# GpSimd's shifted passes as 64-bit additions, squares and normalising multiplies on VectorE

## The chip, the cores and the metric

One core of one Trainium2 chip runs the program. The metric is the device time in microseconds; three runs of the kernel before give 697.55 (696.05 to 713.22). A NeuronCore has TensorE (PE) for matrix products, ScalarE (ACT) for exponentials, VectorE (DVE) and GpSimd (POOL) for elementwise work, and SyncE (SP), whose queue issues the DMAs here. PE writes to PSUM, which has eight banks of 128 x 512 float32; the other operands lie in SBUF.

## The reference

A transformer block with attention and a feed-forward part side by side, both on the same normalised input:

```python
xn = layernorm(x)                         # x: 2048 x 640, no scale or shift
q = (xn @ wq), 32 heads of 20;  k = xn @ wk;  v = xn @ wv     # one k and v for all heads
p = softmax(q k^T / sqrt(20))             # 32 heads x 2048 x 2048
attn = (p v, heads side by side) @ wo
h = relu(xn @ w1 + b1);  ffn = (h * h) @ w2 + b2              # 1536 hidden
return x + attn + ffn
```

The 32 x 2048 x 2048 exponentials are the bulk of the elementwise work.

## The kernel before

The scores are computed transposed: 128 keys on the partitions, 512 queries along the free dimension. A block is four heads (a group) for 512 queries; there are 4 x 8 = 32 blocks. In a block there are 16 tiles of 128 keys, each with four score matrices of 128 x 512, one for each head: 512 tiles, 2048 matrices. The four heads use different rows of PE, so up to four score matrices run side by side as one batch (L1301). The product with v (PV, L1783) has four heads side by side in four column ranges and sums over the tiles of a block in one PSUM bank; v has a column of ones, which gives the sum of the exponentials.

A tile goes one of two ways.

- *ACT's way*: the exponential (L1485) over two or three matrices in neighbouring banks, from PSUM to the ring PT, and then one PV group of four matmuls.
- *VectorE's way*: q is scaled so that a score, plus an offset and converted to a 16-bit integer, is the bit pattern of a bfloat16 power of two with a mantissa that is linear in between (L1581, one conversion for each head, from PSUM into the buffer pbx). The error of the linear mantissa is evened out by four such patterns: the first and three that are shifted by an added 32, 64 and 96 (`PH_D`), each with a weight that lies in its copy of v (`vp`, `PH_W`). A shifted pass adds the constant to all 2048 patterns of a tile (four heads x 512). So the tile has four PV groups. pbx holds ten such sets of patterns.

Of the three shifted passes of a tile VectorE does two (L1602) and GpSimd one (L1664), unless the block is almost over, when VectorE does all (`share` false). A pass that GpSimd does not come to is taken back by VectorE (`S_STEAL`) when more than `PHQ` are queued. GpSimd also squares the ReLU's result (L1094, 48 tiles of 128 x 512) and multiplies the attention's sums by the broadcast reciprocal (L1844, 29 blocks; the last three blocks go another way on VectorE).

VectorE's fast passes from SBUF to SBUF and GpSimd use one port of SBUF, so the program lets GpSimd work only while VectorE reads PSUM. `pieces` and `cut` cut a GpSimd instruction to the length of the VectorE instruction (or two) that it is laid beneath; what is left becomes another piece.

Nothing of this order is decided on the chip. A planner in the file (`Sched`) runs through the whole kernel with a duration for each instruction, picks at each step the request that can start first on each engine (priorities break ties), and writes out a fixed list for each engine with the semaphore waits. Its choices hang on constants: `PHP_F + PHP_E * n` is the planned time of a shifted pass of n patterns on GpSimd; `MAXD` tiles in a block at most go VectorE's way, and `claim` takes one when the rest of the block is longer than `clt` plus VectorE's backlog; `OPN` is how many matrices of claimed tiles may be left when the next one is claimed. `PLAN` holds thirteen further values for each half block: among them `give`, how many of VectorE's matrices may be outstanding, `dstarv` and `hungw`, the backlogs below which a score batch takes more of VectorE's matrices and fewer of ACT's, `await_`, how much later than the batch a PSUM bank may come free and still be counted, and `p1tol`, how late a conversion may be before it is put first. `S_QK` composes the batches from these: two or three matrices for ACT, the rest for VectorE, each in a bank of its own.

```python
if na and len(units) > 2 and len(long_held()) < 4 and not (wanted[0] and pos() < EARLY) and (F >= 5 or F >= 4 and not starving or F == 3 and not hungry):
    a = 3
```

Of the kernel before, what the change touches and what calls it, by code (L numbers as in the profile page):

```python
# [8 lines left out]
I16 = mybir.dt.int16  # L9
ALU = mybir.AluOpType  # L10
# [36 lines left out]
OPN = 1  # L47
# [4 lines left out]
NPB = 10  # L52
PHQ = 2
PHP_F, PHP_E = 156.0, 0.836
OVER = 40.0
# [32 lines left out]
PLAN = [dict(zip(PLAN_KEYS, p)) for p in (  # L88
    (620.0, 3500.0, 600.0, 6000.0, 300.0, 900.0, 12, 1, 0.3, 3, 60.0, 300.0, 4.0),
    (620.0, 3500.0, 600.0, 6000.0, 300.0, 900.0, 12, 1, 0.0, 3, 60.0, 300.0, 1.9),  # L90
    (650.0, 3500.0, 600.0, 6000.0, 300.0, 900.0, 15, 2, 0.0, 3, 0.0, 300.0, 4.0),
    (580.0, 3500.0, 600.0, 6000.0, 300.0, 900.0, 10, 2, 0.0, 3, 150.0, 300.0, 4.0),
    (650.0, 3500.0, 600.0, 9000.0, 300.0, 900.0, 12, 2, 0.0, 3, 60.0, 300.0, 4.0),
    (650.0, 4000.0, 600.0, 6000.0, 150.0, 900.0, 12, 2, 0.0, 4, 0.0, 300.0, 4.0),
    (680.0, 3500.0, 600.0, 6000.0, 300.0, 900.0, 12, 2, 0.0, 3, 60.0, 300.0, 4.0),
    (650.0, 3500.0, 600.0, 6000.0, 300.0, 900.0, 12, 2, 0.0, 3, 60.0, 300.0, 4.0),
    (650.0, 3500.0, 600.0, 6000.0, 0.0, 900.0, 12, 2, -0.3, 3, 60.0, 300.0, 4.0),
    (650.0, 3500.0, 600.0, 6000.0, 0.0, 900.0, 10, 2, -0.3, 3, 60.0, 300.0, 4.0),
    (650.0, 3500.0, 600.0, 6000.0, 0.0, 900.0, 12, 2, 0.0, 3, 60.0, 300.0, 1.9),
    (650.0, 3500.0, 600.0, 6000.0, 0.0, 900.0, 14, 2, 0.0, 4, 60.0, 0.0, 4.0),  # L100
    (760.0, 3500.0, 600.0, 6000.0, 0.0, 900.0, 14, 2, 0.0, 4, 60.0, 0.0, 4.0),
    (760.0, 3500.0, 600.0, 6000.0, 300.0, 900.0, 14, 2, 0.0, 2, 60.0, 600.0, 4.0),
    (760.0, 3500.0, 600.0, 6000.0, 300.0, 900.0, 14, 2, 0.0, 2, 60.0, 600.0, 4.0),
    (620.0, 3500.0, 600.0, 6000.0, 300.0, 900.0, 12, 2, 0.3, 3, 60.0, 300.0, 1.9),
    (650.0, 3500.0, 600.0, 6000.0, 300.0, 900.0, 12, 2, 0.0, 3, 60.0, 0.0, 4.0),
    (650.0, 3500.0, 600.0, 6000.0, 150.0, 900.0, 12, 2, 0.0, 2, 60.0, 300.0, 4.0),
    (650.0, 3500.0, 600.0, 6000.0, 150.0, 900.0, 15, 2, 0.3, 2, 60.0, 300.0, 4.0),
    (650.0, 3500.0, 900.0, 6000.0, 150.0, 1200.0, 12, 2, 0.0, 3, 60.0, 300.0, 4.0),
    (650.0, 3500.0, 600.0, 6000.0, 300.0, 900.0, 12, 2, 0.0, 3, 60.0, 300.0, 4.0),
    (620.0, 2600.0, 600.0, 6000.0, 300.0, 900.0, 12, 2, 0.0, 2, 60.0, 300.0, 4.0),  # L110
    (620.0, 2200.0, 600.0, 6000.0, 300.0, 900.0, 12, 2, 0.0, 2, 60.0, 300.0, 4.0),
    (650.0, 3500.0, 600.0, 6000.0, 300.0, 900.0, 12, 2, 0.0, 3, 60.0, 300.0, 4.0),
    (650.0, 3500.0, 600.0, 6000.0, 300.0, 900.0, 12, 2, 0.0, 3, 60.0, 300.0, 4.0),
    (650.0, 3500.0, 600.0, 9000.0, 300.0, 900.0, 10, 2, 0.0, 3, 60.0, 300.0, 4.0),
    (650.0, 3500.0, 600.0, 9000.0, 300.0, 900.0, 10, 2, 0.0, 3, 60.0, 600.0, 1.9),
    (620.0, 3500.0, 600.0, 6000.0, 300.0, 1200.0, 12, 3, 0.0, 3, 60.0, 300.0, 4.0),
    (650.0, 3500.0, 600.0, 6000.0, 300.0, 900.0, 12, 2, 0.0, 3, 60.0, 300.0, 4.0),
    (580.0, 3500.0, 600.0, 6000.0, 300.0, 900.0, 12, 2, 0.0, 3, 60.0, 300.0, 4.0),
    (650.0, 3500.0, 600.0, 6000.0, 300.0, 900.0, 12, 2, 0.0, 3, 60.0, 300.0, 4.0),
    (650.0, 3000.0, 600.0, 6000.0, 300.0, 900.0, 12, 2, 0.0, 3, 60.0, 300.0, 4.0),  # L120
    (650.0, 3500.0, 600.0, 6000.0, 300.0, 900.0, 12, 2, 0.0, 3, 60.0, 0.0, 4.0),
    (720.0, 3500.0, 600.0, 6000.0, 300.0, 900.0, 12, 2, 0.0, 3, 60.0, 600.0, 4.0),
    (720.0, 3500.0, 600.0, 6000.0, 300.0, 900.0, 12, 2, 0.0, 3, 60.0, 600.0, 4.0),
    (650.0, 3500.0, 600.0, 6000.0, 300.0, 900.0, 12, 2, 0.0, 3, 60.0, 300.0, 4.0),
    (650.0, 2200.0, 600.0, 6000.0, 300.0, 900.0, 12, 2, 0.0, 3, 60.0, 300.0, 4.0),
    (620.0, 3500.0, 600.0, 6000.0, 300.0, 900.0, 12, 2, 0.0, 3, 60.0, 300.0, 4.0),
    (620.0, 3500.0, 600.0, 6000.0, 300.0, 900.0, 12, 1, 0.0, 3, 0.0, 300.0, 4.0),
    (650.0, 3500.0, 600.0, 6000.0, 300.0, 900.0, 12, 2, 0.0, 3, 60.0, 300.0, 4.0),
    (650.0, 3500.0, 600.0, 7500.0, 150.0, 900.0, 14, 2, 0.0, 3, 0.0, 300.0, 4.0),
    (650.0, 3500.0, 600.0, 6000.0, 300.0, 900.0, 12, 2, 0.0, 3, 60.0, 300.0, 4.0),  # L130
    (760.0, 3500.0, 600.0, 6000.0, 300.0, 900.0, 12, 2, 0.0, 3, 60.0, 0.0, 4.0),
    (760.0, 3500.0, 600.0, 6000.0, 300.0, 900.0, 12, 2, 0.0, 3, 60.0, 0.0, 4.0),
    (650.0, 3500.0, 600.0, 9000.0, 300.0, 900.0, 12, 2, 0.0, 3, 60.0, 0.0, 4.0),
    (650.0, 3500.0, 600.0, 6000.0, 300.0, 900.0, 12, 2, 0.0, 3, 60.0, 300.0, 4.0),
    (650.0, 3000.0, 600.0, 6000.0, 300.0, 1200.0, 12, 2, 0.0, 3, 150.0, 300.0, 4.0),
    (760.0, 3500.0, 600.0, 6000.0, 150.0, 900.0, 12, 2, 0.0, 3, 60.0, 300.0, 4.0),
    (620.0, 3500.0, 600.0, 6000.0, 300.0, 900.0, 12, 2, 0.0, 3, 60.0, 300.0, 4.0),
    (720.0, 3500.0, 600.0, 6000.0, 300.0, 900.0, 12, 2, 0.0, 3, 0.0, 0.0, 4.0),
    (620.0, 3500.0, 600.0, 6000.0, 300.0, 1200.0, 12, 2, 0.0, 3, 60.0, 300.0, 4.0),
    (650.0, 3500.0, 600.0, 6000.0, 300.0, 900.0, 12, 2, 0.0, 3, 60.0, 0.0, 4.0),  # L140
    (650.0, 3500.0, 600.0, 6000.0, 300.0, 900.0, 12, 2, 0.0, 3, 60.0, 0.0, 4.0),
    (650.0, 3500.0, 600.0, 6000.0, 150.0, 900.0, 12, 2, 0.0, 2, 60.0, 0.0, 4.0),
    (650.0, 3500.0, 600.0, 6000.0, 150.0, 900.0, 12, 2, 0.0, 3, 60.0, 600.0, 4.0),
    (650.0, 3500.0, 600.0, 6000.0, 300.0, 900.0, 12, 2, 0.0, 3, 60.0, 300.0, 4.0),
    (650.0, 3500.0, 600.0, 6000.0, 0.0, 900.0, 12, 2, 0.0, 3, 60.0, 300.0, 1.9),
    (650.0, 3500.0, 600.0, 6000.0, 150.0, 900.0, 15, 2, 0.0, 3, 60.0, 300.0, 4.0),
    (650.0, 2200.0, 600.0, 6000.0, 300.0, 900.0, 14, 2, 0.0, 3, 60.0, 300.0, 4.0),
    (650.0, 3500.0, 600.0, 6000.0, 300.0, 900.0, 12, 2, 0.0, 3, 60.0, 300.0, 4.0),
    (720.0, 3500.0, 600.0, 6000.0, 300.0, 1200.0, 12, 2, 0.0, 3, 60.0, 300.0, 4.0),
    (650.0, 3500.0, 600.0, 6000.0, 300.0, 900.0, 12, 2, 0.0, 3, 60.0, 300.0, 4.0),  # L150
    (650.0, 3500.0, 600.0, 6000.0, 300.0, 900.0, 12, 2, 0.0, 3, 60.0, 300.0, 4.0),
    (650.0, 3500.0, 600.0, 6000.0, 300.0, 900.0, 12, 2, 0.0, 3, 60.0, 300.0, 4.0),
)]
PAAT = 24.7
PAQ = ()
NPX = 1
PQAT = (7.0, 10.5)
PQSTEP = .3
XRP = 2.0
# [1910 lines left out]
```

## Time and profile before

| | |
|---|---|
| median of the runs | 697.55 us |
| span of the profiled execution | 694.0 us |
| TensorE clock granted | 1.00 throughout |
| exponentials (L1485) | 688: 596 over two matrices, 92 over three |
| conversions (L1581) | 564 instructions for 580 matrices, that is 145 tiles |
| shifted passes on VectorE (L1602) | 302 |
| pieces of shifted passes on GpSimd (L1664) | 510, in 17 lengths |
| squares on GpSimd (L1094) | 85 pieces, 55.4 us |
| normalising multiplies on GpSimd (L1844) | 40 pieces, 32.1 us, and a few more |
| PV matmuls (L1783) | 1468 with PT, 1740 with pbx and vp, 580 with pbx and vx |

The last column of a group's line says how long its engine stood idle just before these instructions and what ended that. A matmul's duration includes the time that it takes to run through PE, so groups of matmuls overlap; what a group costs PE is the distance from its start to the next one's. The same holds to a lesser degree on VectorE: a conversion takes 0.68 us and the next instruction starts 0.60 after it.

### The profile page before, as it was taken

To read this page: it belongs to the slowest core of one execution; us is meant where nothing else is said; L and a number is where in the kernel's file an instruction comes from. 1 tells how busy PE (TensorE), PEld (TensorE's weight loads), DVE (VectorE), ACT (ScalarE), POOL (GpSimd) and SP (SyncE) were. 2 spreads that over 40 slices of the span, in tenths; PEclk is the share of its full clock that TensorE was granted. 3 is DMA by queue.
4 is the path that set the end of the run, shared out by engine and by line. 5 is a ranking of instruction groups with operands and counts; after the bars stand their busy time and mean duration, and the time that the engine had idled before them with its cause. 6 is when DMAs were issued, how large, how long until landed. Compare 5 with 4: busy or idle time off the path is not lost.

```text
span 694.0 us, 23288 instructions
## 1 busy us (share of the span) xinstructions
PE 681.5 (98%) x9825; PEld 222.6 (32%) x9825; DVE 657.9 (95%) x1141; ACT 679.1 (98%) x710; POOL 428.9 (62%) x698
## 2 busy tenths in 40 slices
PE   8999999999999999999999999999999999999997
PEld 5332222222223333332223333333222333333334
DVE  7979999999999999989999999999999999999985
ACT  6999999999999999999999999999999999999995
POOL 2866566766666666667765666676776566655510
PEclk9999999999999999999999999999999999999999
DMA  7362233101101111211100111111110111121001
GB/s 218 77 163 61 61 85 93 29 15 32 24 18 22 33 45 22 47 43 23 26 13 20 44 30 42 33 24 43 28 26 19 22 37 33 31 56 33 12 2 41
DMA packets 39891, 29.89 MB, mean 43 GB/s; under 512 B 23562, under 2 KB 34795, under 8 KB 39787
## 3 DMA queue, kind: packets, MB, share of 16 engines
q1 hardware_dynamic: 39787, 28.39, 17.3%
q8 instruction: 79, 1.29, 0.8%
q14 instruction: 25, 0.20, 0.1%
HBM read 11.12 MB, written 2.62 MB: 20 GB/s over the span
## 4 chain that ended last, share of the span: by engine, by line
PE 59%; ACT 35%; DVE 3%; POOL 1%; DMA 0%; issue 0%; DVEq 0%
ACT PT L1485 35%; PE ps L1783 22%; PE ps L1301 19%; PE ps L950 17%; DVE stats L696 1%; POOL big L731 1%; DVE pbx L1581 0%; DMA pbx<-in_A_x_dram 0%; DVE pbx L1602 0%; POOL vp L1002 0%; DVE hT_tmp L1086 0%; DVE out_sb L1144 0%; POOL pbx L1664 0%; PE ps L939 0%; DVE Rb L806 0%
## 5 line engine op out<-in xcount | busy, mean ns | idle before, releaser
L1485 ACT ACTIVATE PT<-ps 128x1024 bf16<-128x1024 f32 (+1 forms) x688 | 672.4, 1139 | 2.5 <-PE ps L1301 2.3
L1664 POOL TENSOR_SCALAR pbx<-pbx 128x576 int16<-128x576 uint16 (+16 forms) x510 | 314.0, 636 | 173.1 <-DVE pbx L1602 172.0
L1581 DVE TENSOR_SCALAR pbx<-ps 128x512 int16<-128x512 f32 (+1 forms) x564 | 377.3, 696 | 20.1 <-PE ps L1301 18.1
L1301 PE MATMUL ps<-qT,kT 20*128 20x512 bf16 x2048 | 268.7, 384 | 3.0 <-ACT PT L1485 1.4
L1602 DVE TENSOR_SCALAR pbx<-pbx 128x2048 int16<-128x2048 int16 x302 | 206.5, 708 | 1.7 <-POOL big L731 0.8
L1783 PE MATMUL ps<-pbx,vp 128*32 128x512 bf16 x1740 | 157.6, 383 | 1.1 <-POOL vp L1002 0.8
L1301 PEld LDWEIGHTS ps<-qT,kT 20*128 20x128 bf16 x2048 | 67.2, 91 | 259.3 <-ACT PT L1485 185.4
L1783 PE MATMUL ps<-PT,vx 128*32 128x512 bf16 x1468 | 141.6, 383 | 0.2
L950 PE MATMUL ps<-w_sb,big 128*32 128x320 bf16 x1536 | 81.4, 302 | 0.0
L950 PE MATMUL ps<-xnT,w_sb 128*32 128x512 bf16 x960 | 77.1, 384 | 0.5 <-DVE pbx L1581 0.4
L1094 POOL TENSOR_TENSOR big<-hT_tmp 128x256 bf16<-128x256 bf16 (+5 forms) x85 | 55.4, 667 | 22.7 <-DVE pbx L1602 22.2
L1783 PE MATMUL ps<-pbx,vx 128*32 128x512 bf16 x580 | 56.8, 384 | 0.8 <-ACT PT L1485 0.4
L1783 PEld LDWEIGHTS ps<-pbx,vp 128*32 128x32 bf16 x1740 | 41.6, 95 | 48.6 <-issue 33.8
L1783 PEld LDWEIGHTS ps<-PT,vx 128*32 128x32 bf16 x1468 | 37.4, 95 | 43.1 <-issue 33.5
L950 PEld LDWEIGHTS ps<-w_sb,big 128*32 128x32 bf16 x1536 | 31.4, 95 | 32.7 <-issue 25.6
L1844 POOL TENSOR_TENSOR OTs<-Tn,Rb 128x224 bf16<-128x224 f32 (+5 forms) x40 | 32.1, 811 | 15.7 <-DVE pbx L1602 15.7
L1086 DVE TENSOR_SCALAR hT_tmp<-ps,b1col 128x512 bf16<-128x512 f32 x48 | 35.4, 737 | 0.7 <-PE ps L950 0.7
L950 PE MATMUL ps<-wo_p,OTp 120*32 120x320 bf16 (+1 forms) x640 | 34.9, 302 | 0.0
L950 PE MATMUL ps<-xnT,wq_sb 128*32 128x512 bf16 x375 | 31.1, 383 | 0.0
L950 PEld LDWEIGHTS ps<-xnT,w_sb 128*32 128x32 bf16 x960 | 18.9, 94 | 28.8 <-issue 21.1
L1783 PEld LDWEIGHTS ps<-pbx,vx 128*32 128x32 bf16 x580 | 14.9, 94 | 18.3 <-issue 13.1
L1828 DVE COPY Tn<-ps 128x512 f32<-128x512 f32 x29 | 19.7, 680 | 0.1
(95 smaller groups left out, 197.2 us busy)
## 6 DMA issues: line engine op xcount, KB each, us to landing
Rb<-Rr SPq DMA_DIRECT2D x29, 256.0 KB
xres<-in_A_x_dram SPq DMA_DIRECT2D x16, 160.0 KB, 4.1
out_dram<-out_sb SPq DMA_DIRECT2D x16, 160.0 KB, 2.3
qT<-qpk SPq DMA_DIRECT2D x105, 20.0 KB
pbx<-in_A_x_dram SPq DMA_DIRECT2D x3, 640.0 KB
w_sb<-in_B_w_dram SPq DMA_DIRECT2D x1, 1920.0 KB
OTp<-OTs SPq DMA_DIRECT2D x96, 20.0 KB
w_sb<-in_B_w_dram SPq DMA_DIRECT2D x4, 480.0 KB
```

What stands on the lines that cost most here:

```text
L696: v = yield (lambda hh=hh: Req(("dve", 400.0, 470.0, [lambda e: e.bn_stats(out=stats6[:, st, hh, :], in_=x_sb[:, st, 320 * hh:320 * hh + 3 ...
L950: return lambda e: e.matmul(ps[32 * j:32 * j + m, b_[0], 0:n], Lj, R, start=first, stop=last, tile_position=(0, 32 * j))
L1086: v = yield Req(("dve", 658.0, 742.0, [lambda e: e.tensor_scalar(out=hT_tmp[:, k, :], in0=ps[:, b_[0], :], scalar1=b1col[:, f:f + 1], scal ...
L1094: w = yield from pieces(512, 139.0, 1.7, lambda c0, c1: (lambda e: e.tensor_tensor(out=h2T[:, qc % 2, f, c0:c1], in0=hT_tmp[:, k, c0:c1], ...
L1301: ins.append(lambda e, i=i, b=b, t=t, h=h: e.matmul(ps[:, i, :], kT[32 * h:32 * h + DH, t * 128:(t + 1) * 128], qT[32 * h:32 * h + DH, b % ...
L1485: op = yield Req(("act", d_, d_ + 107.0, [lambda e, slot=slot, n=n, src=src: e.activation(out=PT[:, slot:slot + n, :], in_=ps[:, src, :], ...
L1581: return Req(("dve", d_, d_ + 82.0, [lambda e: e.tensor_scalar(out=PB[:, k, hsl, :], in0=ps[:, bk:bk + np_, :], scalar1=OFFS, scalar2=0.0, ...
L1602: return Req(("dve", 600.0, 684.0, [lambda e: e.tensor_scalar(out=PB[:, k, :, :], in0=PB[:, s, :, :], scalar1=PH_D[j], scalar2=None, op0=A ...
L1664: return lambda e: e.tensor_scalar(out=PB[:, k, :, :].rearrange("p h n -> p (h n)")[:, c0:c1], in0=PBU[:, s, :, :].rearrange("p h n -> p ( ...
L1783: ins = [(lambda e, h=h, first=first, last=last: e.matmul(ps[32 * h:32 * h + 32, bk, :], lhs, rhs[h], start=first, stop=last, tile_positio ...
L1828: v = yield Req(("dve", 600.0, 682.0, [lambda e: e.tensor_copy(out=Tn[:, tb, :], in_=ps[:, pvb, :])]), (lambda: None if oldt() is None els ...
L1844: w = yield from pieces(512, 138.0, 2.14, lambda c0, c1: (lambda e: e.tensor_tensor(out=dst[:, c0:c1], in0=Tn[:, tb, c0:c1], in1=Rb[:, a, ...
```

## The change

Four things are changed.

1. A shifted pass on GpSimd is one 64-bit integer addition for each four neighbouring 16-bit patterns (`int64_add`), with the constant repeated in all four; no pattern gets near a carry. Its planned time is 180 + 0.425 n ns. Until the layernorm and the weighted copies of v are done GpSimd keeps to the old form.
2. VectorE does 0.3 of a tile's three passes itself (`DPH`), that is none or one, instead of two; the others are queued for GpSimd, each with its index j.
3. The squares and the normalising multiplies become whole VectorE instructions.
4. The planner's values change: one set for all half blocks (`dstarv` 0, `p1tol` 300, `give` 5, `await_` 150, the rest as most of the 64 sets had them), `OPN` 3, `LATE` 0.5.

```diff
-OPN = 1
+OPN = 3
+I64_F, I64_E = 180.0, 0.425
+DPH = 0.3
+SQ_D, SQP, NM_D, NMP = 330.0, 3, 600.0, 2
-PLAN = [dict(zip(PLAN_KEYS, p)) for p in (
-    (620.0, 3500.0, 600.0, 6000.0, 300.0, 900.0, 12, 1, 0.3, 3, 60.0, 300.0, 4.0),
...
-)]
+PLAN = [dict(zip(PLAN_KEYS, (650.0, 3500.0, 0, 6000.0, 300.0, 300, 12, 2, 0.0, 5, 150, 300.0, 4.0)))] * 64
-LATE = 0.2
+LATE = 0.5
+        PB8 = pbx[:, :].bitcast(U64).rearrange("p (k w) -> p k w", k=NPB)
...
         def sq(qc, f, k, v, old):
-            w = yield from pieces(512, 139.0, 1.7, lambda c0, c1: (lambda e: e.tensor_tensor(out=h2T[:, qc % 2, f, c0:c1], in0=hT_tmp[:, k, c0:c1], in1=hT_tmp[:, k, c0:c1], op=ALU.mult)),
-                                  [v] + old, 1, f"SQ{qc}_{f}")
+            w = yield Req(("dve", SQ_D, SQ_D + 82.0, [lambda e: e.tensor_tensor(out=h2T[:, qc % 2, f, :], in0=hT_tmp[:, k, :], in1=hT_tmp[:, k, :], op=ALU.mult)]),
+                          [v] + old, SQP, f"SQ{qc}_{f}", port=True)
...
                 share = left_ns(b) >= PHT and b < NBLK - 1
-                if share:
-                    php.append((n, b, t, s, acc, left))
-                for j in range(NPH - 1 if share else NPH):
+                own = int((n + 1) * DPH) - int(n * DPH) if share else NPH
+                for j in range(own, NPH):
+                    php.append((n, b, t, s, acc, left, j))
+                for j in range(own):
                     cur = [None]
                     op = yield (lambda: ph_req(cur, n, b, t, s, acc, j))
...
-                def part(c0, c1, k, s):
+                def part(c0, c1, k, s, j, wide):
+                    if wide:
+                        return lambda e: e.int64_add(PB8[:, k, c0 // 4:c1 // 4], PB8[:, s, c0 // 4:c1 // 4], int(PH_D[j]) * 0x0001000100010001)
...
-                    c1 = cut(2048, PHP_F, PHP_E)
+                    wide = have(*[f"VP{c}" for c in range(4)], *[f"X{st}" for st in range(ST)])
+                    F_, E_ = (I64_F, I64_E) if wide else (PHP_F, PHP_E)
+                    n, b, t, s, acc, left, j = php[0]
+                    c1 = cut(2048, F_, E_)
...
-            w = yield from pieces(512, 138.0, 2.14, lambda c0, c1: (lambda e: e.tensor_tensor(out=dst[:, c0:c1], in0=Tn[:, tb, c0:c1], in1=Rb[:, a, c0:c1], op=ALU.mult)),
-                                  (lambda: None if own and free() is None else [done[f"dc{b}"]] + old() + (free() if own else [])), 0, f"N3_{b}")
+            w = yield Req(("dve", NM_D, NM_D + 82.0, [lambda e: e.tensor_tensor(out=dst[:, :], in0=Tn[:, tb, :], in1=Rb[:, a, :], op=ALU.mult)]),
+                          (lambda: None if own and free() is None else [done[f"dc{b}"]] + old() + (free() if own else [])), NMP, f"N3_{b}", port=True)
```

## The prediction

> **What bounds the kernel now.** The page comes first: three engines are busy for nearly the whole span, and a busy share alone cannot say which one paces the rest.
>
> ```profile
> PE 681.5 (98%) x9825; PEld 222.6 (32%) x9825; DVE 657.9 (95%) x1141; ACT 679.1 (98%) x710; POOL 428.9 (62%) x698
> ...
> L1485 ACT ACTIVATE PT<-ps 128x1024 bf16<-128x1024 f32 (+1 forms) x688 | 672.4, 1139 | 2.5 <-PE ps L1301 2.3
> L1664 POOL TENSOR_SCALAR pbx<-pbx 128x576 int16<-128x576 uint16 (+16 forms) x510 | 314.0, 636 | 173.1 <-DVE pbx L1602 172.0
> L1581 DVE TENSOR_SCALAR pbx<-ps 128x512 int16<-128x512 f32 (+1 forms) x564 | 377.3, 696 | 20.1 <-PE ps L1301 18.1
> ...
> L1602 DVE TENSOR_SCALAR pbx<-pbx 128x2048 int16<-128x2048 int16 x302 | 206.5, 708 | 1.7 <-POOL big L731 0.8
> ```
>
> ACT's exponentials stood idle 2.5 us in all, VectorE's conversions 20 us. The table by stretches says that this is so in the steady part too:
>
> ```profile
> 500.00:600.00 100.00, 99.80 (x1482) 32.08 (x1484) 96.00 (x159) 100.00 (x103) 65.46 (x106) 1.00 0.13 28
> ```
>
> (columns: length, then PE, PEld, DVE, ACT, POOL, granted clock, DMA share, GB/s.) PE's 99.80 could be modelled ends, so I read the starts in the timeline of PE:
>
> ```profile
> 501.52 0.39 PE L1301 MATMUL ps<-qT,kT 20*128 20x512 bf16 x3
> 501.85 0.40 PE L1783 MATMUL ps<-pbx,vx 128*32 128x512 bf16 x4
> 502.07 0.60 PE L1783 MATMUL ps<-pbx,vp 128*32 128x512 bf16 x8
> 502.61 0.39 PE L1301 MATMUL ps<-qT,kT 20*128 20x512 bf16 x2
> 502.93 0.40 PE L1783 MATMUL ps<-pbx,vx 128*32 128x512 bf16 x4
> 503.27 0.39 PE L1301 MATMUL ps<-qT,kT 20*128 20x512 bf16 x4
> 503.59 0.61 PE L1783 MATMUL ps<-pbx,vp 128*32 128x512 bf16 x8
> ```
>
> Two PV groups follow each other at 0.22 us; a score batch takes 0.32 to 0.33 us to the next group **whether it holds 2, 3 or 4 matrices**, and the group ahead of it takes 0.32 to 0.34 instead of 0.22. So a batch costs PE 0.32 + 0.10 = 0.42 us however full it is. Groups of 320 columns start 0.14 apart. The ledger: 688 batches (one for each exponential) x 0.42 = 289; PV (1740 + 1468 + 580)/4 = 947 groups, with 240 of FFN, 98 of Q and 15 of K 1300 x 0.22 = 286; 576 groups of 320 columns x 0.14 = 81; 20 us of start. That is 676 of 694: **PE has some 18 us of slack, ACT and VectorE have as little.** All three are bounds at once.
>
> **What one VectorE tile is worth.** Of 512 score tiles 580/4 = 145 go by VectorE's patterns: four conversions (L1581) and three shifted passes, which make four PV groups instead of one. A tile moved from ACT to VectorE saves ACT 4 x 0.43 and costs PE 3 x 0.22 = 0.66 us; it saves PE 0.42 for each batch that goes away. At before's 1468/688 = 2.13 matrices to an exponential a tile takes away 4/2.13 = 1.9 batches, 0.79 us. So freeing VectorE relieves ACT, but PE only by 0.13 us a tile. **PE gains only if batches get fuller.**
>
> **The parts.**
>
> Price of an addition of 2048 patterns on POOL. The trace has no 64-bit addition. The rows nearest to it:
>
> ```profile
> L1664 POOL TENSOR_SCALAR pbx<-pbx 128x576 int16<-128x576 uint16 x153 | 102.2, 670 | 88.0 <-DVE pbx L1602 87.7 <-DVE pbx L1581 0.2
> L1094 POOL TENSOR_TENSOR big<-hT_tmp 128x512 bf16<-128x512 bf16 x11 | 11.4, 1040 | 8.4 <-DVE pbx L1602 8.4
> L1844 POOL TENSOR_TENSOR OTs<-Tn,Rb 128x512 bf16<-128x512 f32 x6 | 7.7, 1276 | 4.8 <-DVE pbx L1602 4.8
> L1664 POOL TENSOR_SCALAR pbx<-pbx 128x2048 int16<-128x2048 uint16 x3 | 5.7, 1897 | 0.7 <-DVE pbx L1602 0.7
> ...
> L1873 DVE TENSOR_TENSOR T<-Tn,rd 128x512 bf16<-128x512 f32 x2 | 1.4, 681 | 0.0
> ```
>
> (1897 - 670)/(2048 - 576) = 0.83 ns an element; starts of neighbours are 36 ns nearer than durations, so a pass is 0.15 + 0.83 x 2048 = 1.86 us. With one such step for each 64-bit element (512 of them) it would be 0.58; with two steps, one for each 4-byte word, 1.00; at the slowest row (L1844 with 320 to 512 elements, 2.1 ns an element) for each word, 2.3. I take the planner's 180 + 0.425 x 2048 = 1.05: next to the two-step figure, and its constants for the three kinds of POOL instruction shown (0.836, 1.7, 2.14 ns an element) are within 3% of their rows.
>
> POOL loses the squares and the normalising multiplies: 55.4 + 32.1 us and smaller groups, about 95. On VectorE the 29 multiplies cost by L1873, whose successor starts 82 ns before its end, 0.60 each: 17 us. The 48 squares have both inputs in SBUF in bf16: at most L1873's 0.60 (29 us), at least 0.16 (L1833's spacing, 8 us); I take the planner's 0.33, 16 us. They wait for FFN's ReLU or a broadcast DMA at the head of VectorE's queue, with conversions behind; POOL's L1844 waited for VectorE alone, never for that DMA, so I cost the wait at nothing. If broadcasts came 1 us late each, it would be 29 us of VectorE.
>
> POOL works only while VectorE does not use the shared port: 172 us of waits behind L1602. The new squares and multiplies block it too.
>
> The Trainium skill, "SBUF — State Buffer", § Who interferes with whom, states that a VectorE instruction with two SBUF inputs contends with a GpSimd instruction that reads SBUF. No run here shows that pair; the planner's order already keeps them apart.
>
> How many passes fit POOL: VectorE's other work is 2.4 us a tile plus some 75 us, about 440 us from the end of the start to the last block; a conversion (0.60) covers half an addition, so additions are mostly cut in two: 1.15 us each. At 90% fill that is 350 of them, against 133 passes now. VectorE keeps 3 x D - 350. Its ledger in 0.60 us slots: 2.4 D + 0.6 (3 D - 350) + 33 + some 38 of waits and port stalls (20 + 18 now), to fit the same 567 us it has now (348 + 181 + 38) less what the kernel gets shorter. With 550: **D = 165, 20 more than now.** Then 4 x (512 - 165) = 1388 matrices stay with ACT, 34 us less of it.
>
> Fuller batches: the planner's values change too (three matrices to ACT whenever four banks are free, banks counted that come free within 150 ns instead of 60, five outstanding VectorE matrices instead of three). ACT's slack frees banks sooner. At 2.13 matrices to an exponential there would be 652 batches, at 2.4 578. What is against more: 8 PSUM banks, of which one or two hold PV sums, one a projection, and five a VectorE backlog could now hold. I take 2.25: 617 batches, 71 fewer.
>
> Sum on PE: 20 x 0.66 = +13, 71 x 0.42 = -30: **-17 us, span 677.** ACT would need 1388 x 0.43 + 617 x 0.06 + 22 = 656, so PE ends last. The planner's 64 sets of values become one; PE's 18 us of slack may grow, and the squares may cost 8 to 29 us, which I leave to the range. No DMA is added, and SP's queue keeps its order. POOL's first 64-bit addition needs its code configured; the row for that is
>
> ```profile
> L664 POOLq MODIFY_POOL_CONFIG  x2: 11/11/11, 1.4 to 1.4; - x2
> ```
>
> followed 0.1 us later by the next POOL instruction, so nothing in the sum. The Trainium skill, "GPSIMD Engine Reference", § 2.1 Instruction dispatch, gives about 6 us for the first call to a freshly loaded kernel; by that the sum would be 683 of span.
>
> The span lies 3.5 us under the median of the runs (697.55). So 677 + 3.5 = **680.5 us**, a gain of 2.4%.
>
> **Rivals.**
> *Fuller still*: 2.4 matrices, 578 batches: -46 + 13 = -33, 664 us. For it: ACT's slack. Against: the banks.
> *Batches do not grow*: 652 batches: -15 + 13, 695 us. For it: PE has no slack, and backlog may eat the banks.
> *The change does not do what it says*: windows under conversions prove too short, VectorE takes most passes back (it steals when more than two are queued). With 200 additions on POOL the ledger gives D = 147: no change, 697 us.
> *Slower*: the addition costs more on the chip than in the order written out by it. The order is fixed, PE's PV queue waits for each pattern in turn. POOL's planned load is 350 x 1.15 + 120 us of blocked port + 25, about 550 of some 615, so 65 us of slack, 0.19 an addition. From 1.25 us for a whole one POOL decides; each 0.1 more adds 35 us; at 1.34 the kernel is 2% slower, at 1.45 it takes 750, at the old 1.86 about 890. For it: no row shows the instruction, and the two ends reach to 2.3. Against: the two-step figure.
>
> **Chances.** Forecast 0.45 (0.08 of it above 683.6), fuller still 0.15, batches do not grow 0.14, not as said 0.10, slower 0.16. 2% (683.6 and 711.5) is about what a measurement of this kernel can tell from no change. Faster 0.37 + 0.15 = 0.52, same 0.08 + 0.14 + 0.10 = 0.32, slower 0.16. The range reaches from inside the fuller case to just over 2% slower, 658 to 715; the POOL bound beyond that is left out.
>
> **What would show it.** Exponentials: about 617 instead of 688, mean above 1139 ns. PV groups with pbx and vx: 660 matmuls instead of 580. L1602's successor: near 145 instead of 302. POOL's additions of 1024 patterns near 0.6 us. PE still without gaps. Wrong if PV's matmuls wait for POOL, or if exponentials stay above 650.

## The result, and the profile after

The changed kernel takes **725.8 us** (median of four runs, 722.8 to 726.8), the kernel before 696.8 in the same session (one of its four runs, at 713.2, was of a slower kind): 1.042 times as long, 95% interval 1.039 to 1.045. The profiled execution has a span of 723.3 us against 694.0. The forecast was 680.5 with a range up to 715, so the sign was wrong and the time lies outside the range.

The same lines of the page as before the change (busy time and share of the span; then line, engine, tiles, count, busy time, mean ns, idle time just before and what ended it):

```profile
PE 695.8 (96%) x9869; PEld 226.4 (31%) x9869; DVE 616.5 (85%) x1075; ACT 678.5 (94%) x696; POOL 382.6 (53%) x686
...
L1425 ACT ACTIVATE PT<-ps 128x1024 bf16<-128x1024 f32 (+1 forms) x674 | 671.7, 1139 | 25.9 <-PE ps L1241 24.1
L1605 POOL INT64_ADD pbx<-pbx x623 | 352.3, 583 | 280.6 <-DVE pbx L1542 169.4
L1521 DVE TENSOR_SCALAR pbx<-ps 128x512 int16<-128x512 f32 x575 | 391.2, 697 | 76.5 <-PE ps L1241 72.5
...
L1542 DVE TENSOR_SCALAR pbx<-pbx 128x2048 int16<-128x2048 int16 x148 | 99.8, 693 | 1.9 <-POOL big L671 1.5
```

VectorE does 148 shifted passes instead of 302 and is busy 41 us less. That time is idle now: 76.5 us ahead of the conversions instead of 20. The exponentials went from 688 to 674, not to 617, and their engine stands idle 25.9 us instead of 2.5.

*Where* the time went is not seen in such sums, but in two other views. The first is the table by stretches (length; busy PE, PEld, DVE, ACT, POOL; granted clock; DMA share; GB/s). Of the changed kernel:

```profile
20.00:50.00 30.00, 26.54 (x311) 8.69 (x307) 23.35 (x64) 26.93 (x34) 22.34 (x36) 0.94 0.40 74
50.00:100.00 50.00, 43.82 (x447) 10.17 (x446) 27.97 (x48) 34.12 (x34) 14.35 (x24) 0.73 0.21 64
...
300.00:400.00 100.00, 99.99 (x1417) 29.93 (x1413) 90.63 (x154) 99.99 (x103) 62.51 (x104) 1.00 0.13 30
...
500.00:600.00 100.00, 99.85 (x1454) 31.23 (x1451) 91.63 (x157) 98.80 (x98) 54.19 (x94) 1.00 0.13 28
```

and of the kernel before:

```profile
50.00:100.00 50.00, 49.43 (x633) 13.74 (x633) 48.36 (x77) 50.00 (x54) 31.34 (x45) 1.00 0.26 67
```

Between 50 and 100 us the changed kernel ran 447 matmuls instead of 633, at a granted clock of 0.73 instead of 1.00. In the stretches from 300 us on shown here, and in those of before, PE and ACT are full to 1.2%.

The second view is **progress**: the start of the n-th score matrix of 2048, read from PE's records of the two executions.

| score matrix | before, us | after, us | difference |
|---|---|---|---|
| first | 10.5 | 17.0 | +6.5 |
| 64th | 36.6 | 45.0 | +8.4 |
| 128th | 60.9 | 85.0 | +24.1 |
| 256th | 101.5 | 132.3 | +30.8 |
| 512th | 184.9 | 214.7 | +29.8 |
| 1536th | 514.8 | 543.8 | +29.0 |
| last | 683.0 | 712.9 | +29.9 |
| end of the span | 694.0 | 723.3 | +29.3 |

All of the loss arises in the first 132 us, and the other four fifths of the kernel run at the pace of before, to 2 us: **the loss does not come from the price of the additions**, which run through the whole kernel. Why the steady part gains nothing is a second question.

The loss has two starts. The source view of the line that builds the identity matrix on GpSimd:

```profile
L604 POOLq MODIFY_POOL_CONFIG  x2: 11/11/11, 1.5 to 1.5; - x2
L604 POOL TENSOR_SCALAR_AFFINE_SELECT ident<-ones_bf x1: 282/282/282, 9.3 to 9.3; 128x128 bf16<-128x128 bf16 x1
...
  issue: 7.9, 1
...
  PE ps L684: 6.2, 1
```

GpSimd is configured at 1.5 us and runs its next instruction at 9.3; before the change this took 0.1 us. PE waits 6.2 us for the identity. The second is the first 64-bit addition, in the timelines of GpSimd and then of PE (start, duration, line, and in brackets the idle time ahead):

```profile
53.23 1.26 POOL L1606 TENSOR_SCALAR pbx<-pbx 128x1280 int16<-128x1280 uint16 x1
60.48 2.21 POOL L1605 INT64_ADD pbx<-pbx  x3 [6.00 <-issue]
```

```profile
54.77 0.61 PE L1727 MATMUL ps<-pbx,vp 128*32 128x512 bf16 x8
61.57 0.62 PE L1727 MATMUL ps<-pbx,vp 128*32 128x512 bf16 x4 [6.18 <-POOL pbx L1605]
62.12 0.61 PE L1241 MATMUL ps<-qT,kT 20*128 20x512 bf16 x3
62.66 0.62 PE L1644 MATMUL ps<-kT,zeros 128*32 128x512 bf16 x4
```

The old and the new form of GpSimd's work need different code; fetching the other took 6.0 us, the order written out knows nothing of it, and PE's queue stands in front of a pattern. The configuration ahead of this wait is recorded at the end of the piece before it:

```profile
L1605 POOLq MODIFY_POOL_CONFIG  x2: 11/11/11, 54.7 to 54.7; - x2
```

What follows costs more than the stop: the score batches behind it are 0.54 us from the next group instead of 0.32, and the table by stretches at a finer cut says why:

```profile
59.00:62.00 3.00, 0.43 (x4) 0.11 (x4) 0.00 (x0) 0.00 (x0) 1.51 (x3) 0.53 0.00 0
62.00:72.00 10.00, 10.00 (x74) 1.84 (x70) 4.06 (x6) 6.14 (x6) 2.91 (x4) 0.50 0.03 8
72.00:86.00 14.00, 14.00 (x108) 2.56 (x106) 6.65 (x11) 8.45 (x9) 2.24 (x3) 0.50 0.14 34
86.00:90.00 4.00, 4.00 (x54) 0.97 (x46) 3.97 (x7) 3.72 (x5) 0.00 (x0) 0.94 0.31 100
```

The granted clock fell to one half at 59.2 us and stayed there for 27.3 us (2.8 + 10 + 14 + 0.5, the edges by their mean), 24.9 of them with PE at work without a gap. Two shorter stretches of half clock, 3.4 us from 45.5 and 6.8 us from 110.4, follow on smaller gaps of PE, 1.4 and 1.7 us.

### The profile page after: what moved, and what is told of

Same layout as the page of the kernel before. It is cut to its first block, busy times and chain, and to the rows that moved or that the text cites. A ratio compares the mean times of both kernels' runs of the same rounds, so it can differ in the third digit from the quotient of the medians.

```text
span 723.3 us, 23198 instructions
## 1 busy us (share of the span) xinstructions
PE 695.8 (96%) x9869; PEld 226.4 (31%) x9869; DVE 616.5 (85%) x1075; ACT 678.5 (94%) x696; POOL 382.6 (53%) x686
## 4 chain that ended last, share of the span: by engine, by line
PE 78%; DVE 9%; ACT 5%; POOL 3%; issue 2%; DMA 2%; DVEq 0%; POOLq 0%
PE ps L1727 28%; PE ps L1241 25%; PE ps L890 24%; ACT PT L1425 5%; DVE pbx L1521 4%; POOL big L671 2%; DVE pbx L1542 2%; DMA Rb<-Rr 1%; DMA Rr<-rd 1%; DVE stats L636 1%; DVE hT_tmp L1026 1%; POOL pbx L1606 0%; PE ps L684 0%; POOL pbx L1605 0%; PE ps L1644 0%
## 5 line engine op out<-in xcount | busy, mean ns | idle before, releaser
L1425 ACT ACTIVATE PT<-ps 128x1024 bf16<-128x1024 f32 (+1 forms) x674 | 671.7, 1139 | 25.9 <-PE ps L1241 24.1
L1605 POOL INT64_ADD pbx<-pbx x623 | 352.3, 583 | 280.6 <-DVE pbx L1542 169.4
L1521 DVE TENSOR_SCALAR pbx<-ps 128x512 int16<-128x512 f32 x575 | 391.2, 697 | 76.5 <-PE ps L1241 72.5
L1727 PE MATMUL ps<-pbx,vp 128*32 128x512 bf16 x1764 | 164.3, 389 | 7.2 <-POOL pbx L1605 6.8
L1727 PE MATMUL ps<-PT,vx 128*32 128x512 bf16 x1460 | 143.8, 390 | 0.6 <-ACT PT L1425 0.5
L1542 DVE TENSOR_SCALAR pbx<-pbx 128x2048 int16<-128x2048 int16 x148 | 99.8, 693 | 1.9 <-POOL big L671 1.5
L890 PE MATMUL ps<-xnT,w_sb 128*32 128x512 bf16 x960 | 81.5, 396 | 0.5 <-ACT PT L1425 0.5
L1727 PE MATMUL ps<-pbx,vx 128*32 128x512 bf16 x588 | 58.3, 389 | 1.1 <-ACT PT L1425 0.7
L1772 DVE COPY Tn<-ps 128x512 f32<-128x512 f32 x29 | 19.8, 682 | 0.3 <-PE ps L1727 0.2
L1034 DVE TENSOR_TENSOR big<-hT_tmp 128x512 bf16<-128x512 bf16 x48 | 19.7, 414 | 0.1
L636 DVE BATCH_NORM_STATS2 stats<-pbx 128x6 f32<-128x320 bf16 x32 | 15.6, 586 | 3.9 <-DMA pbx<-in_A_x_dram 3.9
```

Source lines behind the costliest of these rows:

```text
L636: v = yield (lambda hh=hh: Req(("dve", 400.0, 470.0, [lambda e: e.bn_stats(out=stats6[:, st, hh, :], in_=x_sb[:, st, 320 * hh:320 * hh + 3 ...
L890: return lambda e: e.matmul(ps[32 * j:32 * j + m, b_[0], 0:n], Lj, R, start=first, stop=last, tile_position=(0, 32 * j))
L1034: w = yield Req(("dve", SQ_D, SQ_D + 82.0, [lambda e: e.tensor_tensor(out=h2T[:, qc % 2, f, :], in0=hT_tmp[:, k, :], in1=hT_tmp[:, k, :], ...
L1425: op = yield Req(("act", d_, d_ + 107.0, [lambda e, slot=slot, n=n, src=src: e.activation(out=PT[:, slot:slot + n, :], in_=ps[:, src, :], ...
L1521: return Req(("dve", d_, d_ + 82.0, [lambda e: e.tensor_scalar(out=PB[:, k, hsl, :], in0=ps[:, bk:bk + np_, :], scalar1=OFFS, scalar2=0.0, ...
L1542: return Req(("dve", 600.0, 684.0, [lambda e: e.tensor_scalar(out=PB[:, k, :, :], in0=PB[:, s, :, :], scalar1=PH_D[j], scalar2=None, op0=A ...
```

## The experiments

Three theories were tested one against the other. **Code fetches**: two changes of GpSimd's code, and the clock that follows the second, are the whole loss of the changed kernel. **PE's sum**: PE remains the bound; without the fetches the kernel moves with its batches of scores. Of why the batches did not get fuller, **banks**: time freed on VectorE buys little, since the eight PSUM banks set how many scores can be under way.

### Fetching the old code back at the end

The first fetch of the changed kernel comes before its first 64-bit addition, so the code that the kernel leaves behind at its end must be what the next execution finds. One small instruction of the old form after the last addition tests this:

```diff
+        def S_RESTORE():
+            yield Until(lambda: "PHend" in done and not php and "QKend" in done)
+            yield Req(("pool", 300.0, 300.0, [lambda e: e.tensor_scalar(out=scr[:, 64:96], in0=ones_bf[:, 64:96], scalar1=1.0, scalar2=1.0, op0=ALU.mult, op1=ALU.mult)]),
+                      (lambda: get("ones")), 0, "restore")
```

> The changed kernel with one small 16-bit multiplication on GpSimd after its last 64-bit addition, where GpSimd is idle anyway; the order of all else is the same. Theory 'code loads': GpSimd holds one set of code at a time, the additions leave theirs behind, so the next execution begins by loading the other set (first instruction 7.8 us late, first exponential 6.5 us late); the small multiplication fetches the other set back at the end, where nothing waits. Then the first wait goes and the time falls by 6 to 7 us, to 718 to 720; the stop at 55 us stays. Rival 'worse order' (the lost time lies in the new order and in the additions' price, and the gap at the start is a chance of that execution): no change, 724 to 728.

719.0 us, 1.032 [1.030, 1.035] against before, span 715.9, as expected. The source view of the identity's line now reads

```profile
L605 POOLq MODIFY_POOL_CONFIG  x2: 13/13/13, 1.7 to 1.7; - x2
L605 POOL TENSOR_SCALAR_AFFINE_SELECT ident<-ones_bf x1: 296/296/296, 1.8 to 1.8; 128x128 bf16<-128x128 bf16 x1
```

and the first score matrix starts at 10.4 us again. The second stop stays; GpSimd waits 5.8 us and PE, which comes there later, 2.9. An instruction at the *end* of the kernel makes its *start* 6.6 us shorter (10.4 against 17.0): the code set survives from one execution to the next, and the row of before that showed 0.1 us was that of a kernel that finds its own code there.

### The order told of the second fetch

To this kernel an empty 64-bit addition is added as soon as the old form is done with, planned at 6.1 us, and no other addition comes before it.

```diff
+LIB_NS = 6100.0
...
-                    wide = have(*[f"VP{c}" for c in range(4)], *[f"X{st}" for st in range(ST)])
+                    wide = have("lib")
...
+        def S_LIB():
+            yield Until(lambda: have(*[f"VP{c}" for c in range(4)], *[f"X{st}" for st in range(ST)]))
+            done["lib"] = yield Req(("pool", LIB_NS, LIB_NS, [lambda e: e.int64_add(scr8, ones8, 0)]), (lambda: get("ones")), -2, "lib")
```

> As the run before, and the planner is told of the second load: an empty 64-bit addition, planned at 6.1 us, as soon as GpSimd has done its last instruction of the other set, and nothing planned on GpSimd beneath it. Theory 'code loads': TensorE no longer stops for 6 us at 55 us, so the granted clock stays at 1.0 after it and the 23 us lost between 45 and 110 us go, less what the planner gives up elsewhere for 6 us without GpSimd: 698 to 708. Rival 'worse order': 718 or more, with the clock still down between 60 and 90 us.

711.1 us, 1.022 [1.019, 1.024]. GpSimd still waits 5.6 us for the code, PE does not, the clock is at 0.995 in the mean, and progress is +1.3 us against before at the 128th matrix and +5.0 at the 512th, where the kernel above has +18.5 and +22.4. Up to there both have done the same further work on PE; at the last matrix (+2.2 against +22.5) this kernel has put off 256 matmuls of 320 columns more, 64 groups, 9 us.

A part of the difference is chance: both kernels have a gap of 1.5 us on PE at 37 us, ahead of the fetch, and the half clock behind it lasted 13.7 us above and 3.4 here. In the changed kernel the early stretch was 3.4 us too, and it loses 18.3 us against this kernel from the 64th matrix to the 512th (169.7 against 151.4). So **some 18 us of the loss were an unplanned wait of 6.**

The time is 3 us above the expected range, because the stretch from the last score matrix to the end became 21.1 us long instead of 11.0. That is a second matter, taken up below.

### No fetch at all

From the start GpSimd uses 64-bit additions only; the layernorm's 16 multiplies and the 12 weighted copies of v move to VectorE.

```diff
-XPOOL = tuple(range(16))
+XPOOL = ()
...
+            yield Req(("pool", 200.0, 200.0, [lambda e: e.int64_add(lib8, ones8, 0)]), (lambda: get("ones")), 0, "lib")
...
-            v2 = yield Req(("pool", 235.0 * NPH, 235.0 * NPH + 40.0,
+            v2 = yield Req(("dve", 150.0 * NPH, 150.0 * NPH + 82.0,
...
-                    wide = have(*[f"VP{c}" for c in range(4)], *[f"X{st}" for st in range(ST)])
+                    wide = True
```

> The changed kernel without any load: GpSimd begins with an empty 64-bit addition, so the same set of code stays in place from one execution to the next; the 16 normalisations of x and the 12 weighted copies of v, which need the other set, go to VectorE, and the additions are 64 bits wide from the start. VectorE gets some 9 us more work in the first 45 us. Theory 'code loads': neither wait is there, 697 to 708. Rival 'worse order': 718 or more.

704.3 us, 1.011 [1.009, 1.013], clock 1.0 throughout. The last score matrix starts at 680.5 us, 2.5 *earlier* than before, but 20.6 us are left behind it instead of 11.0. Against before in each session the loss went from 29.0 us to 22.9, 14.9 and 8.1 in the three steps: the fetches are 21 us of it by the time, and the other 8 lie in the last stretch, which the new orders make longer. The identity's instruction follows the 64-bit addition here without a wait (starts at 1.62 and 1.76 us), so not every instruction of GpSimd needs the old form's code.

### Two fetches in the kernel before

The opposite: the kernel before, with nothing of the change in it but one empty 64-bit addition at 46 us, which needs one fetch for itself and one back.

```diff
+        def S_LIB():
+            yield Until(lambda: have(*[f"VP{c}" for c in range(4)], *[f"X{st}" for st in range(ST)]))
+            yield Req(("pool", 200.0, 200.0, [lambda e: e.int64_add(lib8, ones8, 0)]), (lambda: get("ones")), -2, "lib")
```

> The kernel before with one empty 64-bit addition on GpSimd after its last weighted copy of v, in the same written order otherwise: the addition and the next old instruction each fetch their set of code. Theory 'code loads': GpSimd is out for 5.8 + 7.8 = 13 to 14 us at about 46 us, the product with v has to wait for a shifted pass, TensorE stops and its granted clock falls: 15 to 35 us longer, 712 to 732. Rival 'worse order': loads hide in GpSimd's idle time, 696 to 700.

716.1 us, 1.026 [1.022, 1.030]. GpSimd's timeline, the longest wait of PE for it, and the table by stretches while PE works again:

```profile
51.92 0.18 POOL L1997 INT64_ADD libt<-ones_bf  x1 [5.56 <-issue]
58.82 1.76 POOL L1668 TENSOR_SCALAR pbx<-pbx 128x576 int16<-128x576 uint16 x3 [6.72 <-issue]
```

```profile
PE ps L1787 <- POOL pbx L1668: 10.9, 2, 10.6
```

```profile
72.00:81.00 9.00, 9.00 (x73) 1.67 (x71) 4.93 (x9) 5.48 (x6) 4.55 (x7) 0.50 0.18 48
```

(Before runs 122 matmuls in the same 9 us, from a later part of the same order.) Progress is level with before to the 64th matrix, +19.1 us at the 128th, and between +19.7 and +19.8 from the 256th to the last. This gives the price of the slow clock, since order and work are those of before: 19.8 - 10.9 = 8.9 us for 20.9 us of work at half clock (it lasted from 54.2 to 81.5 us, and PE's stop to 60.6), **0.43 us lost for each.** Half a clock didn't cost half the time: a score batch was 0.54 us from the next group instead of 0.32, two groups of 512 columns 0.40 apart instead of 0.23, so the spacing grew by 1.7 to 1.8 and not twofold.

With that price the changed kernel's loss adds up: 6.5 (first fetch) + 6.2 (stop) + 0.43 x (24.9 + 3.4 + 6.8) = 15.1 (clock) is 27.8 of the 29.8 us at the 512th matrix. The other 2.0 I put down to small gaps of the new order, which is not shown.

### The old form in the new order

The changed kernel, with GpSimd's additions in the old form for 16-bit patterns and the planner told so; squares, multiplies and all values as in the change.

```diff
-                    wide = have(*[f"VP{c}" for c in range(4)], *[f"X{st}" for st in range(ST)])
+                    wide = False
```

> The changed kernel with the old 16-bit form of the shifted passes, all else as changed (shares, squares and multiplies on VectorE, planner's values): GpSimd's code is never exchanged. Theory 'code loads': the start runs like that of the kernel before, no stop at 55 us. Theory 'banks': VectorE takes back the passes that GpSimd has no time for, 80 to 110 of them, in time that it did not use, 700 to 708. Rival 'VectorE': the 64-bit form is worth some 90 x 0.6 = 54 us of VectorE, 13 tiles, 23 us of ACT: 715 to 727.

720.1 us, 1.036 [1.030, 1.040]. Neither stop is there, yet in the profiled run, the longest of the four, the clock was at one half for 13.7 us from 38 and 13.7 us from 89, after gaps of 1.4 and 1.7 us that this order leaves by itself (mean clock 0.981; 0.991 and 0.995 in the others); progress is +17.4 us at the 512th matrix. From there to the last it loses 12 us more (+29.5), where the changed kernel loses none. VectorE has 255 passes again, 138 tiles go its way instead of 147, and there are 688 exponentials. So **the 64-bit additions are worth some 12 us over the steady part**, against the old form in the same new setting. The 107 further passes are 64 us of VectorE at 0.60 each; about a fifth of them came out as time. "Banks" (700 to 708) missed, and the time lies where "VectorE" expected it (715 to 727), though the half clock has a part in that.

### Squares back on GpSimd

```diff
-            w = yield Req(("dve", SQ_D, SQ_D + 82.0, [lambda e: e.tensor_tensor(out=h2T[:, qc % 2, f, :], in0=hT_tmp[:, k, :], in1=hT_tmp[:, k, :], op=ALU.mult)]),
-                          [v] + old, SQP, f"SQ{qc}_{f}", port=True)
+            w = yield from pieces(512, 139.0, 1.7, lambda c0, c1: (lambda e: e.tensor_tensor(out=h2T[:, qc % 2, f, c0:c1], in0=hT_tmp[:, k, c0:c1], in1=hT_tmp[:, k, c0:c1], op=ALU.mult)),
+                                  [v] + old, 1, f"SQ{qc}_{f}")
```

> The changed kernel with the squares back on GpSimd in pieces; the additions stay 64 bits wide. GpSimd's list then changes its set of code 94 times. Theory 'code loads': each change costs 5.8 to 7.8 us that the planner does not know, and nearly all of them hold up a product with v: some 94 x 6 = 560 us less what hides, with TensorE's clock at half for most of the span: 1100 to 1500 us. Rival 'worse order': loads hide beside other work, under 800.

1262.5 us in a single run, within the expected 1100 to 1500. From the view of waits (what waited, for whom, total us, times, longest):

```profile
PE ps L1727 <- POOL pbx L1605: 395.3, 45, 24.5
POOL pbx L1605 <- issue: 261.7, 44, 6.9
POOL big L1034 <- issue: 175.4, 25, 7.7
```

Each alternation between squares and additions costs a fetch, in the mean of 5.9 us one way and 7.0 the other (261.7/44 and 175.4/25), and the mean clock falls to 0.74. So the move of squares to VectorE is a condition of the 64-bit form: two kinds of work whose code is not resident together can't alternate on GpSimd 94 times in this kernel.

### One PSUM bank less

The kernel without fetches, with its eighth bank never given out.

```diff
-            bank[7].last = [v]
-            busy[7] = False
+            bank[7].last = None
```

> The kernel without loads (k3_one_lib) with one of PSUM's eight banks left unused after the start. Theory 'banks': a score batch is as full as there are free banks, so the number of free banks and not VectorE's time holds the tiles on VectorE's way at 147 to 150 and the batches at 3.1 matrices; with a bank less both fall (under 125 tiles, more than 740 exponentials) and the time goes up by 40 us or more, to 745 or above. Rival 'VectorE' (the tiles hang on what VectorE has time for): VectorE has the same time, the tiles stay, under 720.

776.3 us in a single run, 72 more than with eight banks:

```profile
L1428 ACT ACTIVATE PT<-ps 128x1024 bf16<-128x1024 f32 (+1 forms) x765 | 732.5, 1146 | 20.8 <-PE ps L1244 20.1
L1524 DVE TENSOR_SCALAR pbx<-ps 128x512 int16<-128x512 f32 (+1 forms) x444 | 309.0, 702 | 151.9 <-PE ps L1244 149.0
```

765 exponentials instead of 664, 114 tiles instead of 150, and VectorE idle 152 us ahead of its conversions, waiting for PE's scores. How full the batches are and how many tiles go VectorE's way hangs on the banks. How much more than on engine time can't be read from this alone: one bank is an eighth of the eight, the load of the next run a thirtieth of VectorE's time, and the planner's values were not chosen for seven.

### VectorE loaded by 20 us more

The kernel without fetches, each square computed twice.

```diff
+            w = yield Req(("dve", SQ_D, SQ_D + 82.0, [lambda e: e.tensor_tensor(out=h2T[:, qc % 2, f, :], in0=hT_tmp[:, k, :], in1=hT_tmp[:, k, :], op=ALU.mult)]),
+                          [w], SQP, f"SQ{qc}_{f}", port=True)
```

> The kernel without loads with each of the 48 squares done twice by VectorE, the second after the first: 48 x (0.33 + 0.08) = 20 us more of VectorE's time in the same eight banks. Theory 'banks': VectorE stands idle for longer than that, so the time changes by no more than the new order's accidents, 700 to 710. Rival 'VectorE': 20 us are 5 tiles, 9 us of ACT, and it is longer by 10 to 20 us: 714 to 724.

707.7 us, 1.017 [1.015, 1.020]: the 48 further squares of 0.41 us are 20 us of VectorE and cost 3.4 us, a sixth (expected by "banks": 700 to 710). At the sixth to a fifth of this run and of the one with the old form, the 41 us that VectorE was handed would be worth 7 to 8 us, an estimate.

### Before's planner values put back, and the new ones alone

The change also replaced 64 sets of planner values by one. Two kernels take this apart: the kernel without fetches with before's values (`PLAN`, `OPN` 1, `LATE` 0.2), and the kernel before with the new ones.

```diff
-OPN = 3
+OPN = 1
...
-PLAN = [dict(zip(PLAN_KEYS, (650.0, 3500.0, 0, 6000.0, 300.0, 300, 12, 2, 0.0, 5, 150, 300.0, 4.0)))] * 64
+PLAN = [dict(zip(PLAN_KEYS, p)) for p in (
+    (620.0, 3500.0, 600.0, 6000.0, 300.0, 900.0, 12, 1, 0.3, 3, 60.0, 300.0, 4.0),
...
-LATE = 0.5
+LATE = 0.2
```

> The kernel without any change of GpSimd's code (704.3 us, 664 exponentials) with before's planner values put back: the 64 sets of values, OPN 1, LATE 0.2; 64-bit additions, squares and multiplies on VectorE stay. The order written out has 707 exponentials and 150 VectorE tiles, 689 us of PE instead of 672. Theory 'values': fuller batches come from the planner's values and not from VectorE's freed time, so here the 43 further batches cost PE 43 x 0.42 = 18 us less the 10 us of slack of its last stretch: 709 to 715 us. Rival 'freed VectorE time fills batches by itself': 700 to 706, as the kernel without code changes.

715.5 us in the median of three runs (a fourth took 732.8), 1.030 [1.027, 1.033], half a us above what "values" expected (709 to 715). More interesting than the time is where it lies: the last score matrix starts at 684.5 us, only 4 later than with the new values, but 29.3 us are left behind it. PE's groups from the last score matrix on, here

```profile
L959 PE MATMUL ps<-w_sb,big 128*32 128x320 bf16 x384 | 14.7, 299 | 0.0
L959 PE MATMUL ps<-wo_p,OTp 120*32 120x320 bf16 x260 | 11.1, 299 | 0.0
```

in the kernel without fetches

```profile
L894 PE MATMUL ps<-w_sb,big 128*32 128x320 bf16 x280 | 10.8, 299 | 0.0
L894 PE MATMUL ps<-wo_p,OTp 120*32 120x320 bf16 (+1 forms) x104 | 4.6, 299 | 0.0
```

and in the kernel before

```profile
L950 PE MATMUL ps<-wo_p,OTp 120*32 120x320 bf16 (+1 forms) x76 | 3.4, 299 | 0.0
L950 PE MATMUL ps<-w_sb,big 128*32 128x320 bf16 x48 | 2.0, 299 | 0.0
```

The second FFN product and the output projection fill PE's free moments, and what finds none is done at the end. Against before 520 more such matmuls are left here (384 - 48 + 260 - 76), 130 groups at 0.14 us: 18.2 us, and the last stretch is 18.3 longer. Without fetches it is 260, 9.1 us, and the stretch is 9.6 longer. **PE's sum is the bound, and the bill comes at the end**: 43 batches more (707 against 664) are 43 x 0.42 = 18 us of PE, its busy time is 16.1 us more, the span 12.7.

> The kernel before with the new planner values alone (one set for all half blocks, OPN 3, LATE 0.5); all of GpSimd's work in the old form. The order written out has 686 exponentials and 138 VectorE tiles (before: 688 and 145), VectorE has 302 shifted passes. Theory 'VectorE and ACT are the bound here': the values keep more matrices for VectorE outstanding, which it has no time for, so tiles go back to ACT: 714.7 + 1.5 + 3.5 = 716 to 722 us. Rival 'the values alone give the fuller batches': 690 to 698 us.

718.4 us, 1.034 [1.030, 1.037], with 686 exponentials, 138 tiles and 302 passes on VectorE: as expected by the theory that VectorE and ACT have no time for these values in the old form. PE here runs 54 groups of multiplications by zeros, which the order puts into gaps to keep PE busy (before: 17). The new values need the 64-bit additions, and the reverse: either without the other is 20 to 23 us slower than before. This kernel loses 17.7 us from the 512th matrix to the last with its squares still on GpSimd, so what the old form lost in the new order can't be put down to the squares on VectorE.

### A set of values for each half block again

The kernel without fetches once more, with 64 sets of values (and `MAXD` 8, `STL` 4500, `PHU` 3000, `DMAXR` 1 instead of 2) searched for this order, as before's were for its own.

```diff
-MAXD = 7
+MAXD = 8
...
-PLAN = [dict(zip(PLAN_KEYS, (650.0, 3500.0, 0, 6000.0, 300.0, 300, 12, 2, 0.0, 5, 150, 300.0, 4.0)))] * 64
+PLAN = [dict(zip(PLAN_KEYS, p)) for p in (
+    (650.0, 1500, 0, 4500.0, 300.0, 300.0, 12, 2, 0, 5, 150.0, 300.0, 4.0),
+    (650.0, 3500.0, 0, 4500.0, 600, 300.0, 16, 2, 0, 2, 150.0, 300.0, 4.0),
...
```

> The kernel without any change of GpSimd's code (an empty 64-bit addition first, the 16 layernorm multiplies and 12 weighted copies of v on VectorE, 64-bit additions throughout) took 704.3 us; this is the same with other planner values, a set for each of the 64 half blocks again, and MAXD 8, STL 4500, PHU 3000, SQP 3. The order written out has 660 exponentials instead of 664 and 148 VectorE tiles instead of 150. Theory 'tail': what that kernel lost against before was the composition of its last stretch (20.6 us from the last score matrix to the end instead of 11.0), which one set of values for all blocks can't repair. Then about 691.1 + 1.5 + 3.5 = 694 to 697 us, level with before (696.0), the last stretch 10 to 14 us, and still no gain in the middle. Rival 'the 64-bit order can't be held on the chip' (waits between engines that the order doesn't foresee): 701 or more. If it were below 688, the PSUM banks would not be the bound that I hold them for.

**692.3 us (692.2 to 693.2), 0.995 [0.993, 0.997]**: 3.4 us faster than before, 12 faster than with one set of values, and the fastest kernel here; 1.7 below the expected 694 to 697. By the 2% bound it is no different from before. It has 660 exponentials and 148 tiles, PE is busy 676.7 us, and the last stretch is 10.3 us:

```profile
PE 676.7 (98%) x9921; PEld 223.5 (32%) x9921; DVE 617.1 (89%) x1107; ACT 672.5 (97%) x682; POOL 378.3 (55%) x683
```

PE's ledger against before: 28 batches fewer, -11.8; 3 tiles more, +2.0; 15 groups of zeros more, +3.3 at 0.22. That is -6.5; PE's busy time fell by 4.8 and the span by 3.5.

## Why the prediction was wrong, step by step

**"Followed 0.1 us later by the next POOL instruction, so nothing in the sum"** is the step that failed most. The row was read as the price of a code change, but it was the row of a configuration that changed nothing, since the execution before had left the same code. The rule that I set beside it and left out, the Trainium skill's "GPSIMD Engine Reference", § 2.1 Instruction dispatch (about 6 us for the first call to a freshly loaded kernel of GpSimd), agrees with this trace at the first addition, 6.0 us; the other fetches took 7.9 at the start and 5.6 and 6.7 back to back in the kernel before with two fetches. Still, the 683 us of span worked out by it were 40 too low. There were two fetches, not one: the first is worth 7.4 us (+29.8 at the 512th matrix against +22.4 with the code restored at the end). The second came unplanned in front of PE, and the clock followed: some 18, as above. A planned fetch, which PE does not wait for, still cost 4 to 5 (+5.0 against +0.8 with none at the 512th matrix, +2.2 against -2.5 at the last, though there the layernorm's multiplies and the copies of v have moved too). Both signs of being wrong came: PE's PV matmuls waited 6.8 us for GpSimd, nearly all of it in this one stop, and the exponentials stayed above 650.

**"20 x 0.66 = +13, 71 x 0.42 = -30: -17 us"**: the prices held, the counts did not. The groups of the changed kernel in its steady part are 0.32 after a score batch and 0.22 after a PV group, as before, and 0.42 for a batch adds up again in the kernels with 660 and 707 of them. But the tiles grew by 2 and the batches fell by 14, at 2.17 matrices to an exponential instead of the 2.25 that I took; the rival "batches do not grow" (2.13) was the nearer. The runs speak for the reason named against fuller batches, the banks, without ruling out the others: from 250 to 600 us the score matrices held 5.0 of the eight banks in the mean before the change (3.69 for ACT, 1.32 for VectorE) and 4.9 after (3.69 and 1.23), each for 1.7 us on ACT's way and 1.3 to 1.45 on VectorE's (from a matrix's start to the end of the instruction that reads it). All uses together, sums and projections too, held 6.8 of the eight banks before and 6.7 after, from the first write to the last read. VectorE's time got free, the banks did not. With one bank less there were 765 batches. That no order with 617 batches exists is not shown; the best that the search over values came to has 660.

**The steady part.** Without fetches and with values of its own the change brings 3.4 us, not 17. Going from 64 sets of values to one, which the prediction left to the range, is a term of its own: without fetches it is 12 us (704.3 against 692.3, with four further values changed). PE as the bound was right: in four kernels without fetches and with eight banks the span is 14 to 19 us longer than PE's busy time (677 to 698 us), and work that found no room earlier is done at the end.

**The price of an addition** was right: by the sizes in the order written out, neighbours start 0.160 + 0.417 ns a pattern apart, 1.01 us for 2048 patterns (taken: 1.05; two-step figure: 1.00), and pieces of 1056 take 0.60 from start to start and last 0.62 (forecast for 1024: near 0.6). So the rival "slower", which had its condition in this price, did not happen. The kernel was slower by another mechanism, which I had not listed among the rivals.

**GpSimd's share**: 290 whole passes in 623 pieces instead of 350; VectorE has 148 passes where 145 were forecast.

**VectorE's prices** were right: a square lasts 0.41 us with the next instruction 0.33 behind its start (taken 0.33), a multiply 0.69 and 0.60 (taken 0.60). The wait for the broadcast DMA, costed at nothing, is 1.7 us in all.

```profile
L1034 DVE TENSOR_TENSOR big<-hT_tmp 128x512 bf16<-128x512 bf16 x48 | 19.7, 414 | 0.1
L1788 DVE TENSOR_TENSOR OTs<-Tn,Rb 128x512 bf16<-128x512 f32 x23 | 15.8, 689 | 1.7 <-DMA Rb<-Rr 1.7
```

## What to carry to other kernels

Before an instruction of a new kind goes on GpSimd, ask which of the kernel's others share its code, and what the execution before has left there: a configuration that took 0.1 us in the old trace says nothing about the new kernel. An order that is fixed beforehand must know of such a wait; 6 us unplanned in front of PE became some 18, planned they became 4 to 5. And time freed on an engine is worth what the resource behind it allows, here a sixth to a fifth of it: see first whether that engine's queue has work that could start, here whether a PSUM bank is free.

## What the runs showed of the hardware

- GpSimd's code for 64-bit additions and that for 16-bit `tensor_scalar` and `tensor_tensor` were not resident together: each change took 5.6 to 8.4 us (shown as "issue" behind a configuration), 44 + 25 such waits in the kernel with squares back on GpSimd. The code that the last instructions of an execution used is what the next execution finds.
- After PE stood still for 6.2 us (and for 10.6 in the kernel before with two fetches) the granted clock was 0.50 for 27.3 us, although PE was busy all the time from 2.4 and 6.4 us of it on. Each microsecond of work at 0.50 cost 0.43 in that kernel.
- How long the half clock lasts is not set by the length of the gap ahead of it. Behind gaps of 1.4 to 1.5 us it lasted 3.4 us (the changed kernel; the fetch told to the planner), 13.7 (the old code back at the end; the old form in the new order) or did not come at all (no fetch, a gap of 1.4 at 83 us); 13.7 us followed a gap of 0.95 in the kernel before with the new values. The stretches named here are one, two, four and eight times 3.41 us. The Trainium skill's "TensorE: Matmul & The Clock Gate", § Part 1, gives some 3.4 us of sustained work until the full clock is back; the trace agrees for the shortest stretches alone. What sets the length of the others is open.
- A 64-bit addition on GpSimd took 0.16 us and 1.67 ns for each 64-bit element on 128 partitions, 0.42 ns a pattern; the 16-bit form took 0.83 ns.
